# Kept rows and the first two experts' weights moved in 512-byte elements, 28 transfers in place of 6

## The chip, the cores and the metric

The kernel runs on one core of a Trainium2 chip. The metric is the device time of one execution in microseconds; the median of several runs is given. Beside it stands one execution taken by the hardware profiler, whose span and trace all views below come from.

## The reference

Two stages follow each other. The first is a gated linear recurrence for each of 4 x 8 heads over 768 tokens of width 48. The second sends each of the 3072 tokens, as a row of 384 numbers, to one of 16 experts (4 groups of 4), chosen by two argmaxes, and scales what the expert returns.

```
f = sigmoid(f_logit)
for t in range(768):
    state = f[t, :, None] * state + outer(k[t], v[t])
    y[t]  = q[t] @ state
x = y as rows (3072, 384)
g = argmax(x @ w_group);  e = argmax(x @ w_expert[g])
out = softmax_g * softmax_e * (relu(x @ w1[g, e]) @ w2[g, e])     # w1: 384 x 1024, w2: 1024 x 384
```

All inputs and the output are float32.

## The kernel before

**First stage.** Tokens are cut into 6 chunks of 128, and a chunk into two halves of two batches, which makes 12 units. Each unit goes through named steps (`load`, `gated`, `multiplied`, `turned`, `scored`, `stated`, `weighed`, `done`, `listed`, `decayed`), and a list of tokens written by hand says in which order steps of neighbouring units stand on every engine. SP (the queue that issues most transfers) loads q, k, v and f of each unit, in elements of 192 bytes.

**Rows.** `listed` turns a unit's results into rows, which the second stage gathers from a table in DRAM, `x_dram`, of 386 numbers (1544 bytes) a row: 384 values, the weight and the token's number. Rows of the first 8 units stay in the SBUF at first, in two tiles called `x_kept`, which borrow the buffers of w2 (tag "w2" of the pool `wp`). `send_kept`, the token "o" in the order of unit 9, sends both to `x_dram` from SP (L758). Rows of the last four units are sent one unit at a time (L750), two from POOL and two from ACT. The function `side` makes that choice; it also sends the small `ends` (L607) of the last two units from ACT. The weight and number of each row (`meta`, L246) are sent by POOL.

**Routing and the early experts.** `route` computes a chunk's choice of experts on DVE. After chunk 3 (`CLOSE`) the counts so far are ranked, and the two fullest experts are loaded at once by `load_early`: two values are read into SP's registers (L377), then SP issues w1 of both, then w2 of both (L381 in `load_layer`). The two w2 wait until the rows kept in their buffers have been sent. When `rows_e` is known, POOL gathers 128 rows for each of the two experts (L393), and the generator `early` runs their passes between the last routing steps: transposes of the gathered rows on PE (`turn_in`, `xg_ps`, L429), the up pass (L439), the down pass (L460).

**Main stage.** When all rows are routed (`choose`), the other experts follow one after the other, with weights loaded up to three passes ahead, and PE works through up and down passes until the end.

**Semaphores.** Transfers issued from SP and ACT draw in turn on eight semaphores. In the built program each such transfer waits for the one that last used its semaphore to land, besides what its data ask for. An engine's queue is in order: what stands behind such a wait stands still too.

Each unit's end on ACT is a chain that PE waits for: `lgT` (L719) is a copy of the scores' product `lT`, which PE then transposes (L722); `xT` (L704) are two copies of the unit's result, which PE transposes into rows (L742) and multiplies with the gates (`lT`, L717).

```
weights, first two experts:
    es = [value(who[0:1, p:p + 1], GE - 1) for p in range(EARLY)]
    w1s, w2s = ([load_layer(wp, e, layer) for e in es] for layer in (1, 2))
order of the last units (l load, o send_kept, d done, r route, x listed, t turned, e early ...):
    NU - 3: "l+2 o d-2 r r x-1 x-1 t t t t b n-1 r g+1 g+1 x-1 r s s s s c+2 w d-1 g+2 w g+2 n m+1 m+1 r n"
    NU - 2: "d-2 r x-1 x-1 r t t t t r g+1 g+1 x-1 s s s s w d-1 w n m+1 m+1"
    NU - 1: "d-2 r r n-1 x-1 x-1 t t t t r x-1 r s s s s w b d-1 w r r"
    NU: "d-2 r e d-1 x-1 x-1 d-1 x-1 r r r e e r e r r e r r e r e r r e e e e e"
```

Of the kernel before, what the change touches and what calls it, by code (L numbers as in the profile page):

```python
# [18 lines left out]
P = 128  # L19
# [4 lines left out]
def kernel(  # L24
# [12 lines left out]
    nc = tc.nc  # L37
    B, H, S, D = q.shape
    N, DM = out.shape
# [29 lines left out]
    wp = ctx.enter_context(tc.tile_pool(name="wp", bufs=2))  # L69
# [4 lines left out]
    w1v = moe_w1.rearrange("g e (ko p) f -> (g e) p ko f", p=P)  # L74
    w2v = moe_w2.rearrange("g e (fo p) d -> (g e) p fo d", p=P)
# [94 lines left out]
    def rows_of(c, s=0, n=B):  # L170

        first = 1 + (c * B + s) * P
        return x_dram[first:first + n * P, :].rearrange("(b p) w -> p b w", p=P)
# [109 lines left out]
    def named(np_, sb):  # L283

        which = sb.tile([1, GE, GE], FP32, tag="which", bufs=1, name="which")[:, 0:np_, :]
        nc.vector.tensor_tensor(which, order[0:1, 0:np_, :], experts[0:1].unsqueeze(1).broadcast_to((1, np_, GE)), OP.mult)
        names = sb.tile([1, GE], FP32, tag="names", bufs=1, name="names")[:, 0:np_]
        nc.vector.reduce_sum(out=names, in_=which, axis=AX)
        nc.vector.tensor_copy(who[:, 0:np_], names)
# [19 lines left out]
    def rank_early(sb):  # L309
        ranks.append(ranked(EARLY, sb))  # L310
# [65 lines left out]
    def value(ap, top):  # L376
        return nc.values_load(ap, engines=(ET.SP,), min_val=0, max_val=top, skip_runtime_bounds_check_because="a table that the routing makes within these bounds")  # L377

    def load_layer(pool, e, layer):
        w = pool.tile([P, KO, F] if layer == 1 else [P, FO, DM], FP32, tag=f"w{layer}", name=f"w{layer}")  # L380
        nc.sync.dma_start(out=w, in_=(w1v if layer == 1 else w2v)[bass.ds(e, 1)].rearrange("o p k f -> (o p) k f"))  # L381
        return w

    def load_weights(pool, ap):
        e = value(ap, GE - 1)
        return load_layer(pool, e, 1), load_layer(pool, e, 2)

    def fetch(pool, rows, n, top=N, late=False):

        w = {"n": n, "pool": pool, "early": top < N, "late": late, "blocks": [(j, min(P, n - j * P)) for j in range((n + P - 1) // P)]}  # L390
        w["x"] = pool.tile([P, len(w["blocks"]), RW], FP32, tag="xg", bufs=2 if pool is ep else 6, name="xg")
        for j, m in w["blocks"]:
            nc.gpsimd.indirect_dma_start(out=w["x"][:, j, :], out_offset=None, in_=x_dram[0:1 + top, :], in_offset=bass.IndirectOffsetOnAxis(ap=rows[:, j:j + 1], axis=0))  # L393
        return w
# [124 lines left out]
    with ExitStack() as fast:  # L519
# [235 lines left out]
        def send_kept():  # L755

            for j, t in enumerate(rows_kept):
                nc.sync.dma_start(out=rows_of(2 * j, 0, 2 * B)[:, :, 0:DM], in_=t)  # L758

        def load_early(pool):  # L760

            rank_early(pool)
            named(EARLY, pool)
            es = [value(who[0:1, p:p + 1], GE - 1) for p in range(EARLY)]
            w1s, w2s = ([load_layer(wp, e, layer) for e in es] for layer in (1, 2))
            weights.update(enumerate(zip(w1s, w2s)))

        def routed(c):
# [34 lines left out]
        def step(nm, i):  # L803
            if nm == "r":
                advance(routes)
            elif nm == "e":
                next(first[0], None)
            elif nm == "p":
                next(pad)
            elif nm == "o":  # L810
                send_kept()
            elif nm == "h":
                next(turning)
            elif 0 <= i < NU:
                if nm == "l":

                    load(i, ("k", "qh"))
                    if i + 1 < NU:
                        load(i + 1, ("f",))
                    load(i, ("v",))  # L820
                    return
                if (nm, i) not in steps_of:
                    steps_of[nm, i] = STAGES[nm](i)
                next(steps_of[nm, i], None)
# [82 lines left out]
    for n in range(GE - 1):  # L907
        w = ws[n]
# [105 lines left out]
    with tc.If(more > 0), ExitStack() as late:  # L1014
# [5 lines left out]
        with tc.For_i(0, last, 1) as i:  # L1020
            w1, w2 = load_weights(wp, b_expert[0:1, bass.ds(i, 1)])
            at = mo.tile([P, 1], FP32, tag="at2", name="at2")
# [12 lines left out]
            w = fetch(ep, row, P, late=True)  # L1035
# [32 lines left out]
```

## Time and profile before

| | us |
|---|---|
| median of 3 timed runs | 421.76 (421.58 to 422.23) |
| the profiled execution | 415.58 |
| its span | 413.8 |
| PE busy | 405.5 (98%) |
| weight loads of PE busy | 374.6 (91%) |
| DVE / ACT / POOL busy | 267.0 / 157.1 / 83.2 |
| SP queue's packets | 125666, 75.5 MB, 62.1% of 16 engines' span |

Times in the views are microseconds from the start of the span. In the timeline a row is: start, length, engine, line, operation, tiles, and in brackets the engine's idle time ahead of it and what ended it. PE is the matrix engine, PEld its weight loads; "ACTq" is a transfer that ACT issues, and its length is that of the issue. Of a DMA stretch the packets, the bytes and the mean rate are given, and how many of the packets were small. The six transfers concerned are issued at 105.30 and 107.9 (kept rows), 111.88, 112.5, 115.34 and 120.5 us (weights); each is 1536 KB. The kept rows land 9.9 and 12.4 us after their issue, the last of the weights 19.8 us.

### The profile page before, as it was taken

What the parts mean: (1) busy time and instruction counts of PE and PEld (TensorE: products, weight loads), DVE (VectorE), ACT (ScalarE), POOL (GpSimd) and SP (SyncE); (2) the same over time, 40 slices, a digit from 0 to 9 for tenths busy, and PEclk for the clock granted to TensorE, in tenths of its full rate; (3) what the DMA queues carried; (4) which work ended last, traced back from release to release, by engine and by line L of the source; (5) the groups of instructions that cost most, each with busy time, mean ns of one, the idle gap of its engine ahead of it and who ended that gap; (6) DMA issues with size and microseconds to landing.
All of it is one profiled execution on the core that took longest, in us unless ns stands there. A gap on an engine that the chain in (4) does not pass through costs nothing.

```text
span 413.8 us, 10066 instructions
## 1 busy us (share of the span) xinstructions
PE 405.5 (98%) x4047; PEld 374.6 (91%) x4047; DVE 267.0 (65%) x778; ACT 157.1 (38%) x353; POOL 83.2 (20%) x127
## 2 busy tenths in 40 slices
PE   8999999999999999999999999999999999999995
PEld 3888888888778978889999999999999999999992
DVE  6666787878898722630899768486595595584230
ACT  6777766666565312221213122222232232231220
POOL 4000010101012157001042221311321320120230
PEclk9999999999999999999999999999999999999999
DMA  9999997877999559974829468486496596485010
GB/s 174 199 202 212 190 185 146 153 141 153 318 346 391 165 192 351 391 276 160 298 68 332 150 230 280 143 326 205 175 349 180 208 347 200 182 320 163 28 47 24
DMA packets 132145, 88.98 MB, mean 215 GB/s; under 512 B 102582, under 2 KB 122748, under 8 KB 132090
## 3 DMA queue, kind: packets, MB, share of 16 engines
q1 hardware_dynamic: 125666, 75.50, 62.1%
q0 software_dynamic: 5792, 11.92, 9.4%
q10 hardware_dynamic: 632, 0.83, 0.6%
q8 instruction: 34, 0.56, 0.5%
q14 instruction: 21, 0.17, 0.1%
HBM read 78.71 MB, written 9.83 MB: 214 GB/s over the span
## 4 chain that ended last, share of the span: by engine, by line
PE 48%; issue 30%; DMA 10%; POOL 6%; DVE 4%; POOLq 1%; ACT 1%; SPq 0%
PE hp L439 12%; DMA out_dram<-yt,xg 7%; PE yo L475 7%; PE ap L659 5%; PE y L701 5%; PE yo L460 4%; POOL out_dram L450 4%; PE cs L600 3%; POOL xg L393 2%; PE x_ps L742 2%; PE ds L676 2%; PE tr_k L634 2%; DMA xg<-x_dram,rows_e 2%; PE tr_q L634 2%; PE y L697 2%
## 5 line engine op out<-in xcount | busy, mean ns | idle before, releaser
L439 PE MATMUL hp<-xe,w 128*128 128x128 f32 (+14 forms) x864 | 138.6, 320 | 0.0
L439 PEld LDWEIGHTS hp<-xe,w 128*128 128x128 f32 x864 | 135.8, 190 | 0.8
L422 DVE STREAM_TRANSPOSE yr<-yT 32x192 f32<-32x192 f32 (+1 forms) x208 | 70.5, 339 | 70.4 <-ACT yT L476 67.8
L475 PE MATMUL yo<-h,w 128*128 128x230 f32 (+13 forms) x672 | 115.8, 333 | 0.0
L475 PEld LDWEIGHTS yo<-h,w 128*128 128x128 f32 x672 | 113.7, 190 | 0.2
L415 DVE STREAM_TRANSPOSE xe<-xg 32x192 f32<-32x192 f32 (+1 forms) x208 | 69.7, 335 | 8.6 <-PE hp L439 5.6
L440 ACT ACTIVATE h<-hp 128x256 f32<-128x256 f32 (+14 forms) x72 | 34.4, 478 | 103.5 <-PE hp L439 103.5
L450 POOL DMA_INDIRECT out_dram<-yt,xg x32 | 34.4, 1076 | 149.2 <-ACT yt L447 143.7
L476 ACT COPY yT<-yo 128x230 f32<-128x230 f32 (+13 forms) x42 | 13.5, 326 | 80.5 <-PE yo L475 80.5
L393 POOL DMA_INDIRECT xg<-x_dram,rows_p x30 | 29.6, 986 | 52.7 <-DMA out_dram<-yt,xg 29.7
L662 DVE TENSOR_TENSOR am<-ap,tri 128x512 f32<-128x512 f32 x48 | 29.8, 682 | 10.8 <-PE ap L659 10.8
L701 PE MATMUL y<-am,v 128*64 128x128 f32 x384 | 24.4, 276 | 0.2
L701 PEld LDWEIGHTS y<-am,v 128*64 128x64 f32 x384 | 20.9, 137 | 3.3 <-issue 1.8
L659 PE MATMUL ap<-Tq,Tk 48*64 48x128 f32 x768 | 23.8, 272 | 0.0
L659 PEld LDWEIGHTS ap<-Tq,Tk 48*64 48x64 f32 x768 | 20.8, 133 | 1.6 <-issue 1.1
L460 PE MATMUL yo<-w,h 128*128 128x384 f32 x64 | 21.3, 486 | 0.0
L460 PEld LDWEIGHTS yo<-w,h 128*128 128x128 f32 x64 | 11.9, 190 | 7.4
L600 PE MATMUL cs<-ld_f,tri 128*128 128x384 f32 x48 | 18.6, 510 | 0.0
L607 POOL DMA_DIRECT2D ends<-eq x10 | 5.4, 541 | 55.5 <-ACT eq L601 55.5
L447 ACT ACTIVATE yt<-yr,xg 128x384 f32<-128x384 f32 (+13 forms) x26 | 14.4, 604 | 5.4 <-DVE yr L422 5.4
L704 ACT COPY xT<-y 128x512 f32<-128x512 f32 x24 | 13.5, 581 | 4.5 <-PE y L701 4.4
L634 PE MATMUL tr_q<-ident,qh 128*128 128x128 f32 x96 | 14.5, 274 | 0.5 <-issue 0.5
(173 smaller groups left out, 369.5 us busy)
## 6 DMA issues: line engine op xcount, KB each, us to landing
w<-in_moe_w_dram SPq DMA_DIRECT2D x34, 1536.0 KB, 11.0
qh<-in_q_dram SPq DMA_DIRECT2D x12, 384.0 KB, 5.3
ld_k<-in_k_dram SPq DMA_DIRECT2D x12, 384.0 KB, 6.0
v<-in_v_dram SPq DMA_DIRECT2D x12, 384.0 KB, 5.8
ld_f<-in_f_logit_dram SPq DMA_DIRECT2D x11, 384.0 KB, 5.8
x_dram<-x_kept SPq DMA_DIRECT2D x2, 1536.0 KB, 11.1
x_dram<-x POOLq DMA_DIRECT2D x2, 384.0 KB, 6.9
x_dram<-x ACTq DMA_DIRECT2D x2, 384.0 KB, 8.1
```

What stands on the lines that cost most here:

```text
L393: nc.gpsimd.indirect_dma_start(out=w["x"][:, j, :], out_offset=None, in_=x_dram[0:1 + top, :], in_offset=bass.IndirectOffsetOnAxis(ap=rows ...
L415: squares(w, lambda n, k_, rk, g, rg: nc.vector.transpose(out=xT[rg, 0:n, k_], in_=x[rk, 0:n, g]))
L422: squares(w, lambda n, k_, rk, g, rg: nc.vector.transpose(out=y[rk, 0:n, g], in_=yT[rg, 0:n, k_]))
L439: nc.tensor.matmul(hp[:, o, :], lhsT=w1[:, ko, (f + o) * P:(f + o + 1) * P], rhs=w["xT"][:, ko, :], start=(ko == 0), stop=(ko == KO - 1))
L440: nc.scalar.activation(h[:, f:f + 2, :], hp, AF.Relu)
L450: sent = nc.gpsimd.indirect_dma_start(out=out, out_offset=bass.IndirectOffsetOnAxis(ap=w["x"][0:m, j, DM + 1:RW].bitcast(U32), axis=0), in ...
L460: nc.tensor.matmul(yp, lhsT=w["h"][:, fo, :], rhs=w2[:, fo, :], start=(fo == 0), stop=(fo == FO - 1))
L475: nc.tensor.matmul(yp, lhsT=w2[:, fo, m * P:(m + 1) * P], rhs=w["h"][:, fo, :], start=(fo == 0), stop=(fo == FO - 1))
L600: nc.tensor.matmul(cs.rearrange("t h d -> t (h d)"), lhsT=tri, rhs=nl[:, b], start=True, stop=True)
L634: nc.tensor.transpose(out=pt[:, a, :], in_=w[nm + "h"][:, b, 2 * a:2 * a + 2, :].rearrange("t r d -> t (r d)"), identity=ident)
L659: nc.tensor.matmul(ap[r][half, a, :], lhsT=w["Tk"][rows, b, a, half], rhs=w["Tq"][rows, b, a, :], start=True, stop=True)
L701: nc.tensor.matmul(ys[b][DP * h:DP * h + DP, a, :], lhsT=w["v"][:, b, 2 * a + (b ^ h), :], rhs=w["am"][b][:, b ^ h, a, :], start=(c == 0 a ...
```

## The change

`load_layer` takes a width `piece`, and when it is given it issues one transfer for every `piece` columns of the tile in place of one for the tile. `load_early` passes 128 (512 bytes). w1 (three rows of 1024 columns in each partition, 4096 bytes each) goes in 8 transfers of 384 elements, w2 (eight rows of 384, 1536 bytes each) in 3 transfers of 1024 elements. `send_kept` does the same with the kept rows: 3 transfers for each tile, each 128 columns of its 1024 rows. So 2 + 2 + 2 transfers become 6 + 16 + 6. All other loads and the later experts' weights stay as they were, and the order of the calls too.

```diff
-    def load_layer(pool, e, layer):
+    def load_layer(pool, e, layer, piece=None):
+
         w = pool.tile([P, KO, F] if layer == 1 else [P, FO, DM], FP32, tag=f"w{layer}", name=f"w{layer}")
-        nc.sync.dma_start(out=w, in_=(w1v if layer == 1 else w2v)[bass.ds(e, 1)].rearrange("o p k f -> (o p) k f"))
+        src = (w1v if layer == 1 else w2v)[bass.ds(e, 1)].rearrange("o p k f -> (o p) k f")
+        n = w.shape[2]
+        for at in range(0, n, piece or n):
+            cols = slice(at, at + (piece or n))
+            nc.sync.dma_start(out=w[:, :, cols], in_=src[:, :, cols])
         return w
...
             for j, t in enumerate(rows_kept):
-                nc.sync.dma_start(out=rows_of(2 * j, 0, 2 * B)[:, :, 0:DM], in_=t)
+                for at in range(0, DM, P):
+                    nc.sync.dma_start(out=rows_of(2 * j, 0, 2 * B)[:, :, at:at + P], in_=t[:, :, at:at + P])
...
-            w1s, w2s = ([load_layer(wp, e, layer) for e in es] for layer in (1, 2))
+            w1s, w2s = ([load_layer(wp, e, layer, P) for e in es] for layer in (1, 2))
```

## The prediction

> **What bounds the kernel now.** I read the busy times first, then the chain of waits, then the stretch from 100 to 150 us, where all six touched transfers run.
>
> ```profile
> span 413.8 us, 10066 instructions
> ...
> PE 405.5 (98%) x4047; PEld 374.6 (91%) x4047; DVE 267.0 (65%) x778; ACT 157.1 (38%) x353; POOL 83.2 (20%) x127
> ```
>
> PE is busy in 98% of the span: what doesn't delay PE costs nothing, and what delays it costs its full length, since after 138 us PE runs without gaps to the last passes. In the chain of waits, the only transfer on the path near the edit is the gather of rows for the first early expert:
>
> ```profile
> 126.47 7.07 DMA xg<-x_dram,rows_e
> 133.68 0.52 PE xg_ps L429 x3
> ```
>
> The timeline of PE says how much of these 7.07 us PE feels: it had other work until 133.2 and waited 0.48 us. And the timeline of ACT shows its work beside this, with the two transfers that it issues itself (ACTq) and its idle time in brackets:
>
> ```profile
> 119.71 0.65 ACTq L607 DMA_DIRECT2D ends<-eq  x1
> 122.45 0.27 ACT L719 COPY lgT<-lT 128x128 f32<-128x128 f32 x1 [2.39 <-PE lT L717]
> 123.46 0.59 ACT L704 COPY xT<-y 128x512 f32<-128x512 f32 x1 [0.74 <-PE y L701]
> ...
> 127.47 0.41 ACTq L750 DMA_DIRECT2D x_dram<-x  x1
> ...
> 130.47 0.17 ACT L644 COPY decays<-gt 128x16 f32<-128x16 f32 x1 [2.15 <-PE gt L643]
> 131.07 0.27 ACT L719 COPY lgT<-lT 128x128 f32<-128x128 f32 x1 [0.43 <-PE lT L717]
> 132.10 0.59 ACT L704 COPY xT<-y 128x512 f32<-128x512 f32 x1 [0.76 <-PE y L701]
> 132.97 0.59 ACT L704 COPY xT<-y 128x512 f32<-128x512 f32 x1 [0.29 <-PE y L701]
> ```
>
> ACT idles after each of its two issues, so it has some 2 to 4 us to give there, and no more: PE's next score and row transposes need its lgT and xT.
>
> The DMA engines are full from 103 to 139 us. Stretches of nearly one packet size give the price of a packet (16 engines, 2 us: 32 us over the count; 160 us over it for the first, which is 10 us long: 50 to 60 us, q, k, v and f in 192 bytes; then 125 to 127, weights in 4096; then 135 to 137, weights in 1536):
>
> ```profile
> DMA packets 10032, 1.94 MB, mean 194 GB/s; under 512 B 10022, under 2 KB 10030, under 8 KB 10030
> ...
> DMA packets 200, 0.81 MB, mean 406 GB/s; under 512 B 1, under 2 KB 2, under 8 KB 200
> ...
> DMA packets 500, 0.76 MB, mean 382 GB/s; under 512 B 3, under 2 KB 500, under 8 KB 500
> ```
>
> These are 15.9, 160 and 64 ns. A line through the first two is 8.8 ns and 36.9 ns per 1000 bytes; it gives 65.5 ns at 1536, so it holds between.
>
> **What the Trainium skill says.** "DMA: Bandwidth & Descriptors", Specifications, names 512 B as the smallest transfer for line rate. No 512-byte stretch is in this trace; the line gives 27.7 ns, 296 GB/s, an estimate well below the 406 of 4096 bytes. The same page, Queues, rings and completion order, says that each engine goes round its queues by packets, of up to 64 descriptors: the smaller SP's pieces, the sooner the queues of POOL and ACT come to their turn. The trace agrees in part: the gather of 126.47 had next to no packets on the POOL queue (1 by 130.9) until a whole layer had passed, then 119 from 131.0 to 133.6, side by side with SP and ACT. The same page, Why a DMA increments its semaphore by 16 and not by 1, asks for one semaphore per transfer in flight. This program has eight for SP and ACT together, in turn, so the ninth transfer waits for the first to land. That such a wait is real is seen on POOL: a gather (L393), which shares no data with a result's scatter, waited for its landing 8 times (29.7 us).
>
> **The change, part by part.** Nothing changes on PE, DVE, ACT and POOL but waits. SP issues 22 transfers more: kept rows 2 to 6, w1 2 to 16, w2 2 to 6.
>
> *Bytes.* Kept rows: 2048 packets of 64 ns become 6144 of 27.7; over 16 engines 8.2 us become 10.6, +2.4. w1: 768 of 160 ns become 6144, 7.7 to 10.6, +2.9. w2: as kept rows, +2.4. In all +7.7 us of DMA time. The last w2 landed at 140.3 and lands at about 148. Its first use is the second early expert's down pass; the 64 matmuls of both begin at 147.7, so about 152. The engines are idle from 140 to 149.6, so the next loads are not delayed. w1 was in by 127 and is needed at 136.2 and 142.2; by the sums below it is in by 136, and PE now waits for one block of columns at a time. w2 of the first is then at about 140, for 147.7. So the 7.7 us themselves are hidden behind slack of 4 us and more; without it they would cost in full.
>
> *SP's issues.* One weight load takes 0.6 us of SP (111.88 to 112.5), 22 more about 14 us. Behind them on SP stand only further pieces, then a value (L377) that waits for DVE until 147.3. A w1 piece moves in 384 x 27.7 / 16 = 0.66 us, so SP just keeps up. Nothing on PE pays, if it does.
>
> *The gather's wait goes.* It starts when kept rows, x and meta have landed, and comes through sooner: about 124 and in by 128. PE gains up to 0.5 us; the next limit there is ACT's second xT (133.56) ahead of lT at 134.12.
>
> *The added waits, on ACT.* In the built order, the second "ends" transfer took a semaphore last used by an old load; now it is the last kept piece's. ACT's first x (L750) waited for the first kept transfer (landed 115.2); now for piece 5 of the second w1. Both stand in ACT's queue, and all ACT work behind stands still.
> - Last kept piece: kept packets ended at about 119.3 before, +2.4, and +1.0 since POOL's x of 115.9 (0.39 MB at 390 GB/s; it moved after 121) now gets in ahead: 122.7, and 0.7 to land (as 119.6 to 120.3): 123.4. ACT then needs 0.65 to issue and 0.27 for lgT before xT, which may start 0.2 later than 123.46 before PE feels it: free up to 122.65. Cost 0.75 us.
> - Piece 5 of w1: 122.7, plus 13 pieces x 0.66 = 8.6, plus 1.1 for both gathers (0.39 MB) that now come first, plus 0.7: 133.1. After it come 0.41, 0.17, 0.27 and twice 0.59, with gaps 2.2 us, until lT may start: 135.3 against 134.12, **1.2 us** late. This holds the 0.75 and the lost gain within it (0.75 - 0.5 is less), it isn't added.
> - ACT's second x (136.40) waits for the last w1 piece: 133.1 + 3 x 0.66 = 135.1, no cost.
>
> Both ends of the unknown price: the faster stretch of 192-byte packets (103 to 105 us: 2343, 13.7 ns) makes 512 bytes 25.7 ns, and each ns moves piece 5 by (6144 + 4992)/16, 0.7 us: 131.7, 0.2 us early, and the kept piece at 122.65, free. A gain up to the 0.5 us is thus not excluded. If 512 bytes cost 33 ns (unaligned rows in x_dram of 1544 bytes, columns of w1 4096 apart; nothing here shows either), it is 136.8, +4.9 us. I take 27.7, the line's value. Sum on the profiled execution: 415.58 + 1.2 = 416.8. The median of the timed runs is 6.2 us above the profiled execution; I carry the 1.2 over: **423.0 us**.
>
> **The rivals.**
> - *ACT's waits end in time and the gather's wait goes*: not slower. For it: ACT's idle time before lgT (2.39) and decays (2.15), and a price of 25.7 suffices. It decides from piece 5 landing before 131.9; below 131.4 the whole 0.5 us is won: 421.3. Against it: the sum lands 1.2 us later. If timed runs have longer gathers than the profiled one, over 0.84 us could be won.
> - *Small pieces move slowly*: 33 ns, or SP feeding a piece in 0.94 us only (13 x 0.28 = 3.7 more): +4.9 us, 426.7. Against it: the line fits three sizes.
> - *The change does nothing*: hardware that cuts elements anyway. The trace shows 4096-byte packets, so hardly; 421.8.
>
> **How the numbers follow.** A measurement here can tell 0.2%, 0.84 us. Forecast 0.40, mostly +0.84 to +3; rival one 0.35, of it 0.10 past -0.84; slow pieces 0.20; nothing 0.05. Slower: 0.40 + 0.20, less 0.02 of the forecast's low edge, 0.58; faster 0.10; within 0.32. The range, 421.0 to 426.8, leaves out most of the 0.10 and the upper half of slow pieces. The forecast's own range is 422.3 to 425.
>
> **What would show it.** Packets: 4864 go, 18432 come: 145713, and 137084 under 2 KB. A stretch near 119 us with 27.7 ns a packet. ACT's "ends" issue at about 123.4 instead of 119.71, its first x at 133 instead of 127.47, gathers landed by 128, PE's wait for lT in place of xg_ps. If ACT's issues stay where they were and the time still grows, or w1 is what PE waits for, the steps are wrong.

## The result, and the profile after

| | before | after |
|---|---|---|
| median on one chip, 5 runs each | 421.76 us (420.75 to 423.00) | 429.23 us (428.78 to 429.77) |
| ratio | | 1.0175, 95% interval 1.0152 to 1.0198 |
| the profiled execution | 415.58 us | 429.77 us |
| its span | 413.8 us | 427.9 us |

The change costs 7.5 us where 1.2 were forecast. Line numbers after the change are 5 or 6 higher: `ends` is L612, lgT L724, lg L727, x L755, the kept rows L764, the gather L398, xg_ps L434, hp L444.

The head of the page after, the granted clock in 40 slices, and the count of packets:

```profile
span 427.9 us, 10130 instructions
...
PE 410.7 (96%) x4047; PEld 378.9 (89%) x4047; DVE 266.9 (62%) x778; ACT 156.7 (37%) x353; POOL 83.0 (19%) x127
...
PEclk9999999999996999899999999999999999999999
...
DMA packets 146065, 88.98 MB, mean 208 GB/s; under 512 B 102934, under 2 KB 137436, under 8 KB 146010
```

The bytes are those of before. The packets are 352 more than forecast, which is 16 small ones for each of the 22 added transfers. PE has the same 4047 matmuls, but 5 us more of busy time: a part of them ran at a lower clock, in the slices that show 6 and 8. PE's share fell from 98% to 96%, so it also waited. The chain of waits (start, length, what) says for what:

```profile
116.32 13.38 DMA x_dram<-x_kept
...
129.78 0.65 ACTq L612
...
130.47 0.28 ACT lgT L724
...
130.79 0.48 PE lg L727
```

In the chain shown before, this place held no kept rows. The last piece of the kept rows lands at 129.7; only then does ACT issue `ends`, which stood at 119.71 before, and only after that comes lgT. The timeline of ACT and of PE, idle time before the instruction in brackets:

```profile
130.47 0.27 ACT L724 COPY lgT<-lT 128x128 f32<-128x128 f32 x1 [10.47 <-DMA x_dram<-x_kept]
...
130.79 0.48 PE L727 MATMUL lg<-ident,lgT 128*128 128x128 f32 x1 [6.57 <-ACT lgT L724]
```

ACT stood still for 10.5 us. PE had work for four of them and then waited 6.57 us. Last, PE in stretches of 5 us (busy time, instructions, granted clock, DMA share, GB/s):

```profile
120.00:125.00 5.00, 4.23 (x114) 1.00 1.14 221
125.00:130.00 5.00, 0.00 (x0) 0.94 1.19 184
130.00:135.00 5.00, 4.20 (x19) 0.50 1.16 303
135.00:140.00 5.00, 5.00 (x126) 0.87 1.15 305
```

After the pause PE ran at half its clock until about 136: four transposes tr_q took 1.06 us instead of 0.60. The Trainium skill, "TensorE: Matmul & The Clock Gate", Part 1, says that the clock halves after at least one idle window of some 3.4 us and comes back after as long a busy stretch; the 6.6 us of idling and the 0.50 agree. In a run below, with rows 2048 bytes apart, a stop of only 2.78 us was followed by a low clock too, so here less than the page's 3.4 us was enough.

The sum at the first full stretch of hp: it began at 142.23 before and at 150.85 after, 8.6 us later. Of these 6.6 are the wait and 0.5 come off, since the gather's wait has gone; the remaining 2.5 fit the slower clock. The other 5.5 us by which the two spans differ come from a later gap in PE, from 172 to 177, which goes with the chip and not with the change, as the second look at the changed kernel shows below.

Why the last piece came so late is in the transfers. Two stretches after: kept rows alone (111 to 117), then w1 alone (129 to 131), both in 512-byte elements:

```profile
DMA packets 2443, 1.24 MB, mean 207 GB/s; under 512 B 43, under 2 KB 2442, under 8 KB 2442
...
DMA packets 1245, 0.61 MB, mean 306 GB/s; under 512 B 51, under 2 KB 1245, under 8 KB 1245
```

Sixteen engines for 6 us, over 2443, is 39 ns a packet for the store, and it varies: 55 ns from 117 to 119, 38 from 119 to 121, 56 from 125 to 127. The load takes 32 us over 1245, 25.7 ns. The engines are as full in one as in the other.

### The profile page after: what moved, and what is told of

The parts are those of the page before. It is cut to its first block, busy times and chain, and to the rows that moved or that the text cites. A ratio compares the mean times of both kernels' runs of the same rounds, so it can differ in the third digit from the quotient of the medians.

```text
span 427.9 us, 10130 instructions
## 1 busy us (share of the span) xinstructions
PE 410.7 (96%) x4047; PEld 378.9 (89%) x4047; DVE 266.9 (62%) x778; ACT 156.7 (37%) x353; POOL 83.0 (19%) x127
## 4 chain that ended last, share of the span: by engine, by line
PE 46%; issue 29%; DMA 10%; POOL 6%; DVE 2%; another core or an unknown queue 2%; ACT 1%; POOLq 1%; DVEq 1%; SPq 1%; ACTq 0%
PE hp L444 11%; DMA out_dram<-yt,xg 7%; PE yo L480 6%; PE ap L664 4%; PE y L706 4%; POOL out_dram L455 4%; PE cs L605 3%; DMA x_dram<-x_kept 3%; PE x_ps L747 3%; PE yo L465 2%; POOL xg L398 2%; PE tr_k L639 2%; PE tr_q L639 2%; PE ds L681 2%
## 5 line engine op out<-in xcount | busy, mean ns | idle before, releaser
L444 PE MATMUL hp<-xe,w 128*128 128x128 f32 (+14 forms) x864 | 141.4, 323 | 2.5 <-issue 1.8
L444 PEld LDWEIGHTS hp<-xe,w 128*128 128x128 f32 x864 | 137.5, 192 | 4.5 <-issue 2.4
L398 POOL DMA_INDIRECT xg<-x_dram,rows_p x30 | 29.5, 984 | 52.7 <-DMA out_dram<-yt,xg 30.0
L612 POOL DMA_DIRECT2D ends<-eq x10 | 5.4, 541 | 55.6 <-ACT eq L606 55.6
L639 PE MATMUL tr_q<-ident,qh 128*128 128x128 f32 x96 | 15.4, 286 | 0.7 <-issue 0.6
L639 PE MATMUL tr_k<-ident,kh 128*128 128x128 f32 x96 | 15.1, 284 | 0.0
```

Of the source, the lines that this page charges most:

```text
L444: nc.tensor.matmul(hp[:, o, :], lhsT=w1[:, ko, (f + o) * P:(f + o + 1) * P], rhs=w["xT"][:, ko, :], start=(ko == 0), stop=(ko == KO - 1))
L639: nc.tensor.transpose(out=pt[:, a, :], in_=w[nm + "h"][:, b, 2 * a:2 * a + 2, :].rearrange("t r d -> t (r d)"), identity=ident)
```

## The experiments

**Theory.** Stores of 512 bytes into `x_dram` are slow, because its rows lie 1544 bytes apart and a piece begins at any multiple of 8 bytes. The last piece then lands late, ACT stands before `ends`, PE before lg. **Rivals.** It is ACT's wait alone that costs, and the slow store would be hidden without it; it is the weights' pieces; it is the number of transfers; any 512-byte store is slow. Ratios are to the kernel before on the same chip; its median was 416.91 us in the first group, 416.88 in the second and 421.96 in the third.

**The kernel before once more** gives a trace to compare with.

> The kernel before once more, for a trace from the same chip as the other runs. The timed runs of before stand 6.2 us above its profiled execution. If the second gap of the changed kernel (PE from 172.5 to 176.4 us, with DVE waiting 9.6 us on an unknown queue) is nothing of the change, this trace should show such a gap too, and a span near 420 us; if the gap belongs to the change, it is absent here and the span is near 414.

It took 417.05 us. The gather was issued at 127.94, and PE waited for it:

```profile
135.13 0.52 PE L429 MATMUL xg_ps<-ident,xg 128*128 128x128 f32 x3 [1.44 <-DMA xg<-x_dram,rows_e]
```

So the wait that the change takes away is 0.5 us in one trace of before and 1.4 in another. Against this trace, where the first full stretch of hp begins at 143.69, the changed kernel is 7.2 us late there and not 8.6; the medians differ by 7.5. PE has no gap near 173 here, which at this point spoke for the change as the cause of that gap.

**Kept rows alone in pieces.**

```diff
-            w1s, w2s = ([load_layer(wp, e, layer, P) for e in es] for layer in (1, 2))
+            w1s, w2s = ([load_layer(wp, e, layer) for e in es] for layer in (1, 2))
```

> Only the kept rows are sent in 512-byte pieces; the four layers go whole. Theory 1 (stores of 512 bytes into the rows of x_dram are slow, 43 to 58 ns a packet, so the last kept piece lands near 129.7): the store is as slow here. But the second ends transfer of ACT now reuses the semaphore of the first kept piece (landed near 113), so ACT does not stop; what stays is the gather, which needs the kept rows and lands near 135, and PE waits some 2 us for it: +1.5 to +3 us. Rival (the weights' pieces are what is slow): kept pieces alone cost next to nothing, 0 to +0.5 us.

Measured: 424.23 us, ratio 1.0151 (1.0113 to 1.0189), nearly the whole loss, where 3 us at most were expected. But ACT's `ends` went out at 119.84 and its x at 127.61: ACT was not held. The timelines of POOL and of PE show another path:

```profile
134.53 1.06 POOL L398 DMA_INDIRECT xg<-x_dram,rows_e  x1 [14.45 <-DVE val L233]
...
136.10 2.40 PE L706 MATMUL y<-am,v 128*64 128x128 f32 x19 [2.82 <-issue]
...
140.62 0.88 PE L434 MATMUL xg_ps<-ident,xg 128*128 128x128 f32 x3 [1.72 <-DMA xg<-x_dram,rows_e]
```

The gather reads `x_dram`, so it waits for the kept rows. It was issued 6.6 us later than in the kernel before. The releaser that the profile names, DVE's val, ended just before, at 134.4; but in the run with ACT's transfers on POOL, below, the gather goes out before val begins, so it does not need val. The last kept piece landed at 133.5, later than all else that the gather reads. PE then waited 1.72 us for the gathered rows. The clock was 0.57 from 135 to 140.

For PE's stop before y the profile names no releaser. The trace has a hint: PE stops after the 13th of 32 matmuls, and goes on 1.37 us after the end of a packet of 16 KB on the queue that the profile calls `instruction` (134.73). In the run with ACT's transfers on POOL it stops after the same matmul, and again goes on 1.37 us after that packet (134.16). In the second trace of before the packet ended at 130.66, before PE came to this matmul. So PE may have waited for its own instructions, delivered late by full DMA engines; no run tests this.

**Weights alone in pieces.**

```diff
-                for at in range(0, DM, P):
-                    nc.sync.dma_start(out=rows_of(2 * j, 0, 2 * B)[:, :, at:at + P], in_=t[:, :, at:at + P])
+                nc.sync.dma_start(out=rows_of(2 * j, 0, 2 * B)[:, :, 0:DM], in_=t)
```

> Only the four layers are moved in pieces of 512 bytes; the kept rows go whole. Theory 1: loads of 512 bytes are near 26 to 29 ns a packet, the kept rows land by 121, ACT's second ends transfer waits about 1 us within its idle time, and piece 5 of the second w1 lands by 130.5: -0.5 to +0.3 us. Rival (the weights' pieces are slow): most of the loss of 7.5 us stays, above +4 us.

Measured: 415.75 us, ratio 0.9977 (0.9965 to 0.9989): faster, by about 1 us. The time of this half of the change is what the prediction's rival "ACT's waits end in time" says. ACT's first x went out when piece 5 of the second w1 had landed, and PE no longer waits for the gather (timeline of ACT, then of PE):

```profile
132.35 0.41 ACTq L755 DMA_DIRECT2D x_dram<-x  x1
...
133.44 0.33 PE L727 MATMUL lg<-ident,lgT 128*128 128x128 f32 x1
133.60 0.49 PE L434 MATMUL xg_ps<-ident,xg 128*128 128x128 f32 x3
```

So the whole loss lies in the kept rows.

**The change with all of ACT's transfers on POOL**, so that no transfer on ACT shares the semaphores.

```diff
-            return nc.gpsimd if i < NU - 2 else nc.scalar
+            return nc.gpsimd
```

> The changed kernel with the ends and the rows of the last two units issued by POOL in place of ACT, so that no transfer of ACT waits for a semaphore of SP's pieces. Theory 1 (ACT's queue stands behind the last kept piece): PE no longer stops at 124 to 131 and its clock stays up; the store is still slow, so the gather lands near 135 and PE waits about 2 us: +2 to +3.5 us against before, in place of +7.5. Rival (PE waits for the gather or the weights anyway, ACT's stop is only beside it): +6 us or more stays.

Measured: 424.73 us, ratio 1.0164 (1.0128 to 1.0200). ACT was never held and the loss stayed. (A later stop of PE, 1.59 us at 165.68, is new and adds to this trace.) My idea that ACT's stop decides falls: with ACT free the gather, issued at 133.56, brings the same loss, with PE stopping before y for 2.73 us and then before xg_ps (timeline of POOL, then of PE):

```profile
133.56 1.06 POOL L398 DMA_INDIRECT xg<-x_dram,rows_e  x1 [12.96 <-DMA w<-in_moe_w_dram]
...
139.71 0.87 PE L434 MATMUL xg_ps<-ident,xg 128*128 128x128 f32 x3 [2.61 <-DMA xg<-x_dram,rows_e]
```

Two paths lead from the last kept row to PE, and either is enough.

**The change with rows of x_dram 1600 or 2048 bytes apart.** Every piece then begins at a multiple of 64 or of 512 bytes. The pad is filled with zeros and stored with `meta`.

```diff
-    RW = DM + 2
+    RW = 400        # 512 in the other kernel
```

> The same with rows 1600 bytes apart: every piece begins at a multiple of 64 bytes, though not of 512. Theory A with a unit of 64 bytes: as with 2048, 26 to 30 ns a packet, loss under 0.5%. Theory A with a larger unit (128 to 512): in between or still slow, 35 to 50 ns a packet, loss 0.7 to 1.8%. Theory B: 40 to 58 ns, loss 1.5 to 2%.

> The changed kernel, but the rows of x_dram lie 2048 bytes apart instead of 1544 (the pad is filled with zeros), so every 512-byte piece of a kept row begins at a multiple of 512 bytes. The gather then moves a third more bytes per row, x and meta are stored as before. Theory A (a 512-byte store is slow only because rows at multiples of 8 bytes make it begin and end inside a unit of the memory): the kept pieces take 26 to 30 ns a packet as the loads of w1 do, the last lands near 123, ACT issues 'ends' near 123.4 and stands still under 1 us, the gathers are issued by 128; time 416 to 419 where before is 417 (a loss of at most 0.5%, pad and gather in it). Theory B (any store in elements of 512 bytes is slow, or it is the number of transfers): 40 to 58 ns a packet as in the changed kernel, last piece near 130, loss 1.5 to 2%.

The stretch from 111 to 117 with 1600 bytes, against the 2443 packets of after in the same stretch, and the one from 111 to 119 with 2048:

```profile
DMA packets 3291, 1.68 MB, mean 279 GB/s; under 512 B 47, under 2 KB 3290, under 8 KB 3290
...
DMA packets 4804, 2.42 MB, mean 303 GB/s; under 512 B 124, under 2 KB 4803, under 8 KB 4803
```

That is 29.2 ns a packet, and 26.6 ns with 2048 bytes. The theory holds: size, number and order of these stores are those of the change, and only where a row begins differs. Most of it is won at 64 bytes. (The distance between rows changes with their beginnings; the two were not tried apart.) The Trainium skill, "DMA: Bandwidth & Descriptors", How a descriptor splits into AXI transactions, says, of reads, that a descriptor not starting at a multiple of 256 bytes costs extra beats. Three quarters of the pieces at 1600 don't start there, and with them the mean is only 2.6 ns above that of 2048; that rule is not the main cause here.

The time of 1600: 419.26 us, ratio 1.0067 (1.0037 to 1.0097), with single runs from 416.35 to 422.76. The trace is of the fastest of these seven, and it is the prediction come true; timeline of ACT and then of PE:

```profile
122.46 0.65 ACTq L614 DMA_DIRECT2D ends<-eq  x1
...
132.83 0.41 ACTq L757 DMA_DIRECT2D x_dram<-x  x1
...
133.68 0.33 PE L729 MATMUL lg<-ident,lgT 128*128 128x128 f32 x1 [1.28 <-ACT lgT L726]
```

`ends` was forecast for 123.4, x for 133.1, PE's wait for 1.2 us; the gather went out at 124.38, forecast for 124. The median run lost about twice the forecast, and has no trace. With 2048 the same wait in PE's timeline was longer:

```profile
136.39 0.33 PE L729 MATMUL lg<-ident,lgT 128*128 128x128 f32 x1 [2.78 <-ACT lgT L726]
```

And the clock paid too, as the stretch of 5 us around it shows (columns as above):

```profile
135.00:140.00 5.00, 3.61 (x28) 0.66 1.10 298
```

It took 420.87 us, 1.0119 (1.0085 to 1.0153). Both kernels lost more than the 0.5% that I expected at most. Their gathers and the stores of `meta` carry the pad as well, and with 2048 x went out at 135.47 instead of 132.83. Of that, 1.2 us are a shift that PE's lT before it has too (122.45 against 121.24); whether the pad is the reason for the rest was not tried apart. So aligned rows gave back the price of the packets, but only a part of the time: 1.66 to 1.75% of loss became 0.67 and 1.19%.

**The kernel before with its kept rows in six transfers of whole rows.**

```diff
-                nc.sync.dma_start(out=rows_of(2 * j, 0, 2 * B)[:, :, 0:DM], in_=t)
+                for lo, hi in ((0, 3), (3, 6), (6, 8)):
+                    nc.sync.dma_start(out=rows_of(2 * j, 0, 2 * B)[:, lo:hi, 0:DM], in_=t[:, lo:hi])
```

> The kernel before, with the kept rows in six transfers instead of two, but of whole rows (3, 3 and 2 blocks of 128 rows each; packets of 1536 bytes, at rows of 1544). The number of transfers and SP's issue time are those of the change, the size of the element is that of before. If the size of the element (with its alignment) is the cause, packets stay at 60 to 70 ns, the last kept rows land near 120, time within 0.5 us of before. If the number of transfers is the cause, the store ends some 5 us later and the time is up by 5 us or more, as with the kept rows alone in pieces (1.5%).

Measured: 416.88 us, ratio 1.0001 (0.9992 to 1.0011), 67 ns a packet (1438 from 111 to 117). The number of transfers costs nothing.

**Kept rows in two halves of 768 bytes**, at rows of 1544, otherwise the kernel before.

```diff
-                nc.sync.dma_start(out=rows_of(2 * j, 0, 2 * B)[:, :, 0:DM], in_=t)
+                for at in range(0, DM, DM // 2):
+                    nc.sync.dma_start(out=rows_of(2 * j, 0, 2 * B)[:, :, at:at + DM // 2], in_=t[:, :, at:at + DM // 2])
```

> The kernel before, with the kept rows in pieces of 768 bytes (two transfers for each tile) at rows of 1544. Aligned price by the line: 8.8 + 36.9 x 0.768 = 37 ns a packet, 4096 packets, 9.5 us on 16 engines, 1.3 us more than before. If an unaligned packet pays a fixed 17 ns more, as the 512-byte pieces do: 54 ns, 13.8 us, last piece near 125, ratio 1.003 to 1.010. If the loss is a matter of pieces of 512 bytes only, 37 to 40 ns and within 0.3% of before.

The stretch from 111 to 117:

```profile
DMA packets 2106, 1.61 MB, mean 268 GB/s; under 512 B 32, under 2 KB 2105, under 8 KB 2105
```

45.6 ns a packet; ratio 1.0027 (1.0013 to 1.0040). Neither of my two numbers, 54 and 37 to 40, was right.

**The kernel before with rows of 1600 bytes**, kept rows whole.

> The kernel before, with the rows of x_dram 1600 bytes apart instead of 1544 (pad filled with zeros, kept rows whole). Whole rows at multiples of 8 bytes took 66 ns a packet, weights of the same 1536 bytes 64 to 70. If each packet that begins or ends inside a unit of 64 bytes pays the same 17 ns or so that the 512-byte pieces lose by it, aligned whole rows take 50 ns. If the unaligned ends cost whole rows little, it stays at 62 to 66. Time: kept rows land at most 2 us earlier, which only the gather's wait of 0 to 1.4 us feels: ratio 0.997 to 1.001.

Measured: 421.34 us, ratio 0.9985 (0.9971 to 0.9998). The stretch from 111 to 115 here, and the one from 111 to 117 in the second trace of the kernel before:

```profile
DMA packets 942, 1.44 MB, mean 359 GB/s; under 512 B 19, under 2 KB 940, under 8 KB 940
...
DMA packets 1403, 2.15 MB, mean 358 GB/s; under 512 B 16, under 2 KB 1402, under 8 KB 1402
```

That is 67.9 ns a packet, against 68.4 unaligned. A whole row pays nothing for its place. So the loss is no fixed sum for each packet: it is some 10 to 30 ns at 512 bytes, 9 at 768 (against the line's 37) and none at 1536. Between 111 and 117 that would fit a packet that takes no less than some 40 to 46 ns when it is stored unaligned, with larger ones slower than that by their bytes alone. But the stretches at 55 and 56 ns lie above such a floor, and with the kept rows alone in pieces one reached 92 ns (349 packets from 125 to 127). What makes the price vary stays open.

**The changed kernel once more**, on the third chip.

> The changed kernel once more, on the chip that runs the others of this group. In its first trace PE lost 6.6 us before lg and about 2 us to the clock, and then 4 us more from 172 to 176 us, which the kernels with only the kept rows in pieces did not show. If those 4 us belong to the change, they are seen here again: span 427 to 428, ratio 1.025 or more where before is 416.9. If they belong to the chip of the first comparison (where before was also 5 us slower, 421.76), PE has no such gap here, and the ratio is 1.015 to 1.02, 423 to 425 us.

Measured: 428.51 us, ratio 1.0166 (1.0132 to 1.0200), and 37 ns a packet (2627 from 111 to 117). The wait before lg was 6.04 us, and the late gap was there again, in hp:

```profile
173.52 0.48 PE L444 MATMUL hp<-xe,w 128*128 128x128 f32 x2 [1.14 <-issue]
```

But the three others that ran on this chip, none with stores of 512 bytes, have such a gap in the same pass, at their own time. In PE's timeline of the kernel before with rows of 1600 bytes (its line numbers are 2 higher than those of before):

```profile
164.86 0.38 PE L441 MATMUL hp<-xe,w 128*128 128x128 f32 x2 [1.14 <-issue]
...
166.97 5.50 PE L441 MATMUL hp<-xe,w 128*128 128x128 f32 x17 [1.12 <-issue]
```

In the traces from the two chips where the kernel before takes 416.9, with the small stores or without, PE has no such stop for "issue" there. So the gap goes with the chip and not with the change; what PE waits for in it the profile does not say. In the kernel with rows of 1600 bytes its stops add up to 2.8 us, and the clock is at half for 6.8 us from 166.1 on, which costs 3.4 more. These 6.2 us are a little more than what that chip is slower by (421.96 against 416.9). They would also explain the 6 us by which the first chip's runs of before lay above its profiled execution, which has no gap; that this execution was on another chip is not on record.

**Two tries to beat both kernels:** the weights in pieces with whole kept rows, once with ACT's transfers on POOL, once with rows of 1600 bytes.

> The weights of the change in pieces, kept rows whole as before, and the two x and one 'ends' transfers that ACT issues given to POOL. With the weights alone in pieces the ratio was 0.9977: the gather's wait on PE was gone, ACT's first x was issued at 132.35 and PE waited there. If ACT's stop there is still felt by PE, giving the transfers to POOL wins 0.3 to 0.8 us more (ratio 0.996 to 0.997). If POOL's queue, which issues the gathers behind them, delays the gathers instead, the gain of about 1 us is lost (ratio 1.000 or above).

> The weights in pieces as in the change, kept rows whole, and rows of 1600 bytes. With the weights alone in pieces at rows of 1544 the ratio was 0.9977. If aligned rows bring the kept rows and the gather in earlier, the gather is not what PE waits for any more, so no further gain: 0.997 to 0.999. If the alignment helps the gathers and the x stores too, 0.995 to 0.997.

Measured: 0.9984 (0.9975 to 0.9993) and 0.9981 (0.9967 to 0.9996). Neither is better than the weights alone in pieces, 0.9977, by more than the intervals. That half of the change is the version to keep; it is worth about 1 us.

## Why the prediction was wrong

- **The price of a kept packet, 27.7 ns: the step that failed.** The line came from loads alone. For loads it held (25.7 ns for w1). The stores took 39 ns from 111 to 117 and up to 56 later. The sum named the cause, rows of 1544 bytes, and let it count for 33 ns at most, since the trace of before had no store of 512 bytes. It did have unaligned ones, the whole rows, which pay nothing for their place; that they are no measure for pieces is what the halves show.
- **"Kept rows +2.4"** thus became about 8.7, the other terms of that sum left as they were: the last piece landed at 129.7, not 123.4. All other steps were dated from it.
- **ACT's first added wait, 0.75 us:** the mechanism was right, to the queue, the semaphore and the instruction behind it. With the last piece 6.3 us later, PE's wait was 6.6 us. With aligned rows `ends` went out at 122.46, in time by the sum's own limit of 122.65, and PE did not wait. In the changed kernel the wait also shows the shared semaphores: `ends` has no data of the kept rows, and went out 0.08 us after the last of them had landed. The wait that the prediction read on POOL does not show them: the scatter takes its row numbers from a tile `xg`, and the gathers fill such tiles in turn, so the two do share data.
- **The second added wait, 1.2 us for piece 5 of w1:** at 1600 bytes and with the weights alone x stood where forecast (132.83 and 132.35 against 133.1). PE waited 1.28 us in the first and not at all in the second. After the change it came at 139.95 and cost nothing, since PE was by then late itself.
- **The clock was left out.** An idle PE was priced at its length. Single waits of 1.28 to 1.6 us left the clock alone; waits of 2.78 and 6.57 us were followed by 0.66 and 0.50. Some 2.5 of the 8.6 us are this.
- **The gather's wait goes:** so it did where kept rows stayed whole (1 us faster). With aligned pieces the gather went out at 124.38, as dated. With unaligned ones it was issued later instead, 130.77 against 126.47. I did not see it as a second path by which the same late store reaches PE. The runs with ACT free show that nearly the whole loss comes without ACT's stop: there PE waits for the gather last, and the clock falls.
- **Carrying the sum from the profiled execution to the median** did no harm: the change costs 1.0175, 1.0166 and, for its kept rows alone, 1.0151 times the time of before on three chips, with the late gap and without it.
- **The rival "small pieces move slowly"** had the right cause and the wrong size: 426.7 against 429.23. As a rival it put the slowness on the loads too, and with that on w1's piece 5; it was the stores alone.

## What to carry to other kernels

Before a store to DRAM is cut into pieces of 512 bytes, look at the pitch of its rows: at multiples of 8 bytes a piece cost 37 ns and more, at multiples of 64 it cost 29, and whole rows of 1536 bytes cost the same in both. Here a price from loads did not hold for unaligned stores, and whole rows gave no sign of what pieces of them would cost. When a transfer becomes late, follow everything that waits for it, by data and by shared semaphore, before pricing one path; and add what the clock takes where PE stands still: here stops of 2.8 us and more did it, single ones of 1.6 us did not, and in the chip's late gap several stops of 0.2 to 1.1 us within 4 us did it together.

## What the runs showed of the hardware

The Trainium skill, "DMA: Bandwidth & Descriptors", Specifications, asks for at least 512 bytes for line rate and says that smaller transfers are read, modified and written back. Here 512 bytes were not enough for it: aligned they moved at 279 to 306 GB/s, where weights in 4096 bytes had 406, and stored unaligned at 139 to 223 in the two traces of the changed kernel. Whether the memory reads and writes back the ends of an unaligned piece was not seen. Against my expectation, a fixed surcharge for each unaligned packet does not fit: it was 9 ns at 768 bytes and none at 1536.
